# Batch 0 in two head sets and two token parts, one PSUM pool placed by hand, W_in's product in chunks, and a new order of all work

## The chip, the core and the metric

The kernel runs on one core of a Trainium2 chip. The metric is the device time of one execution in microseconds.

## The reference, cut to what matters

```python
def sm_attn(qq, kk, vv):
    s = scale * np.matmul(qq, kk.transpose(0, 1, 3, 2))
    a = np.exp(s - np.max(s, axis=-1, keepdims=True))
    a = a / (np.sum(a, axis=-1, keepdims=True) + 1e-09)
    return np.matmul(a, vv)

p_packed = sm_attn(p, k, v)              # p: 8 batches, 8 heads, 32 rows, 64 wide
out = sm_attn(q, p_packed, p_packed)     # q, k, v: 8 batches, 8 heads, 576 tokens, 64 wide
x = out.transpose(0, 2, 1, 3).reshape(4608, 512)
r = np.maximum(x @ w_in, 0.0)            # w_in: 512 x 2048
g = s * (r * r) + b                      # s, b: one number each
return g @ w_out                         # w_out: 2048 x 512
```

All inputs are fp32 in HBM. The first attention packs the 576 keys and values of a head into 32 rows; the second attends from the queries to these 32 rows.

## The kernel before

All loads of q, k, v, p and the weights are issued by GpSimd (POOL), whose DMA turns fp32 into bf16 on the way. The output's stores and the DMA transposes are issued by SyncE (SP). TensorE (PE), VectorE (DVE), ScalarE (ACT), POOL and SP each keep the order in which the program text names their instructions. That order is written out by hand as a string of words, which `run` turns into calls. For batch b the words are:

- Lk, Lq, Lv, Lp, Lwi, Lwo, Lpall, Lsb: loads of k, q, v, p, of a block of W_in's columns, of a quarter of W_out's rows, of the p of batches 2 to 7 at once, and of s and b.
- Tk, Tq: transposes of k and q by PE (batches 0 and 1), by halves of the heads. Dk, Dq: the same by DMA transpose (batches 2 to 7). PD, PP, PA, PPA: p is doubled and transposed into `pbd`.
- F: first scores and their exp, one of two head sets `a` at a time (heads 2g + a). V: v is put into the order of `vr` by DVE. P: the packed values with their sums, `pps`, then a reciprocal and two scalings into `pk`. X: `pk` transposed into `ppd`.
- S: second scores and exp (`e2`). A: column sums with `onesbd`, then ln and exp(-x) on ACT for the reciprocals, then the product on DVE, into `aT`.
- W: `ppd` times W_in, in chunks of 512 of W_in's 2048 columns, cast into `pw`. The attention's second product is folded into it: x @ W_in is `aT` times `pw`.
- M (h for the halves in batch 0): 128 columns of the hidden layer for all 576 tokens, four products of 288 columns, then a relu (ACT, sometimes DVE) and a square (DVE) into `gT`.
- O: steps of 512 output columns for 128 tokens, sixteen steps to an output tile (`yps`). At the sixteenth DVE multiplies by s, adds the bias row `biasrep`, and SP stores.
- BT, BC: W_out's column sums (16 products on 32-row strips), and a fp32 product with `rowsf` that adds the four strips and spreads them over the partitions, times b, into `biasrep`.
- Z, Y: products of a zero tile `zb`, results unused. Z goes to a tile of its own (`zps`), Y into the tile that the next step will use.

PSUM has two pools: `psh` (two buffers of two banks, tag h: scores, transposes, W pairs, M) and `psy` (four buffers of one bank: outputs, packed values, single W chunks). Which buffer a step gets follows from the order of requests. An M step occupies one `psh` buffer until its relu has read it.

Batch 0 goes by halves of 288 tokens and by halves of the heads. Its words:

```python
        Lwi0 Lwi1 Lwo0 Lwi2 Lwi3 Lwo1 Lp1 Tk0.0 Z10 PD Tk0.1 Lk1 PP0 Z3 F0.0 V0.0 F0.1 Z5 P0.0 V0.1 Lv1
        P0.1 Z1 Tq0.0 Z1 X0 Z1 Tq0.1 Lq1 Lwo2 Lwo3 Lpall Z3 S0 Z3 A0.0 Z1 W0.0 A0.1 G0.0 E Y8 h0.0.0
        G0.1 Z1 h0.2.0 Z1 W0.1 Y4 h0.2.1 Y1 h0.0.1 Y1 M0.4 M0.5 W0.2 M0.6 M0.7 W0.3 M0.8 M0.9 M0.10
```

Later batches interleave M steps of batch b with O steps of the batch before, mostly one or two of each in turn. In the profile nearly every ACT, DVE and POOL instruction bears line 73 and every matmul line 62 (transposes 65), the lines of the helpers that record them, so groups are told apart by the names of their tiles: hps is a `psh` tile, wps a single W chunk, rlu a relu's result.

Of the kernel before, what the change touches and what calls it, by code (L numbers as in the profile page):

```python
# [14 lines left out]
def kernel(  # L15
# [32 lines left out]
    JJ = NP // 16  # L48

# [8 lines left out]
    psh = ctx.enter_context(tc.tile_pool(name="psh", bufs=2, space=bass.MemoryType.PSUM))  # L58
    psy = ctx.enter_context(tc.tile_pool(name="psy", bufs=4, space=bass.MemoryType.PSUM))
# [17 lines left out]
    early = []  # L77

    def big(dt=F32):
        if early:  # L80
            return early.pop()
        return psh.tile([P, 2, NB if dt == F32 else 2 * NB], dt, tag="h", name="hps")
# [12 lines left out]
    pn = [constp.tile([P, 2, 2, D], BF16, name=f"pn{i}") for i in range(2)]  # L95
    pall = constp.tile([16 * (B - 2), 16, 2, D], BF16, name="pall")
# [10 lines left out]
    rowsf = constp.tile([P, P], F32, name="rowsf")  # L107
# [7 lines left out]
    def load(what, b, h0=0, h1=H):  # L115
        src = {"k": k, "q": q, "v": v}[what]
        if h0 == 0:
            raw[what, b] = rawp.tile([R, H, NC * D], BF16, tag=what + "n", name=what + "n")
        pool.dma_start(
            out=raw[what, b][:, h0:h1, :],  # L120
            in_=src[b, h0:h1].rearrange("h (r c) d -> r h (c d)", c=NC),
        )

# [21 lines left out]
    def load_sb():  # L145
        sp.dma_start(out=svec[:], in_=moe_s[0:1].unsqueeze(0).to_broadcast([P, 1]))
        sp.dma_start(out=bvec[:], in_=moe_b[0:1].unsqueeze(0).to_broadcast([P, 1]))
# [6 lines left out]

    def prep_p(b):
        pt = big(BF16)
        for x in range(2):
            tr(
                pt[:, 0, x * P:(x + 1) * P],
                pn[b][:, x, :, :],  # L160
                identb[:],
            )
        for c2 in range(2):
            act.copy(
                out=pbd[D * c2:D * c2 + D, :, b, :, c2, :],
                in_=pt[D * c2:D * c2 + D, 0, 0:2 * P].rearrange("p (g a j) -> p a g j", g=4, a=2),
            )

    def prep_pall():
        n = 16 * (B - 2)  # L170
        pts = [psy.tile([P, 8 * P], BF16, tag="y", name="pps") for _ in range(2)]
# [6 lines left out]
        for x in range(2):  # L178
            src = pts[x][:].rearrange("p (t n) -> p t n", n=P)[:, :, 0:n].rearrange(
# [9 lines left out]
    def on_pe(b, what, half):  # L189
        dst = (kT if what == "k" else qT)[b % 2]  # L190
        if what == "q":
            dst = dst[:].rearrange("p h c r -> p (h c r)")
        tpw = big(BF16)
        tp = [tpw[:, 0], tpw[:, 1]]
        split = b == 0 and what == "q"
        if split:
            tp[1] = psy.tile([P, 2 * NB], BF16, tag="y", name="tps")
        for h4 in range(4):
            for cp in range(CP):
                o = (h4 % 2) * HS + cp * R  # L200
                tr(
                    tp[h4 // 2][:, o:o + R],
                    raw[what, b][:, 4 * half + h4, cp * P:(cp + 1) * P],
                    identb[0:R, 0:R],
                )
        d = dst[:, half * 4 * HS:(half + 1) * 4 * HS].rearrange("p (a s) -> p a s", a=2)
        if split:
            act.copy(out=d[:, 0], in_=tp[0][:, 0:2 * HS])
            vec.tensor_copy(out=d[:, 1], in_=tp[1][:, 0:2 * HS])
        else:  # L210
            vec.tensor_copy(out=d, in_=tpw[:, :, 0:2 * HS])
# [8 lines left out]
    def order_v(b, h0=0, h1=H):  # L220
        vec.tensor_copy(
            out=vr[:, :, h0:h1, 0:D].rearrange("r c h d -> r h c d"),
            in_=raw["v", b][:, h0:h1, :].rearrange("r h (c d) -> r h c d", c=NC),
        )

    def first_scores(b, a):
        if a == 0:
            e1[b] = attp.tile([R, 2, NC, 4, NP], BF16, tag="e1", name="e1")
        s1 = big()
        for g in range(4):  # L230
            for cp in range(CP):
# [8 lines left out]
                )  # L240
        act.activation(
# [8 lines left out]
    def packed(b, half=None):  # L250

        if not half:
            pps[b] = psy.tile([P, NB], F32, tag="y", name="pps")
        pp = pps[b][:, 0:2 * DV].rearrange("p (a x) -> p a x", a=2)
        for a in range(2):
            for c in range(NC):
                for g in range(4) if half is None else (2 * half, 2 * half + 1):
# [8 lines left out]
        if half == 0:  # L266
            return
        rd = smp.tile([P, 2], F32, tag="rd", name="rd")
        vec.reciprocal(out=rd[:], in_=pp[:, :, D])
        pk[b] = smp.tile([P, 2, 2, D], BF16, tag="pk", name="pk")  # L270
        for a in range(2):
# [6 lines left out]
    def turned(b):  # L278

        pt = pps[b][:, NB // 2:].bitcast(BF16)  # L280
        for a in range(2):
            tr(pt[:, a * P:(a + 1) * P], pk[b][:, a].rearrange("p c d -> p (c d)"), identb[:])
        vec.tensor_copy(
            out=ppd[b % 2][:].rearrange("p a g j -> p (a g j)"),
            in_=pt[:, 0:2 * P],
        )

    def second_scores(b, by_half=False, with_w=False):
        e2[b] = attp.tile([P, 2, S], BF16, tag="e2", name="e2")
        tiles = [big() for _ in range(2)]  # L290
        for a in range(2):
            for g in range(4):
                for c2 in range(2):
                    t, i = (c2, a) if by_half else (a, c2)
                    mm(
                        tiles[t][NP * g:NP * g + NP, i, 0:HS],
# [6 lines left out]
        if by_half:  # L303
            exp_half(b, tiles, 0, 0)
            exp_half(b, tiles, 1, 0)
            s2[b] = tiles
            return
        if with_w:
            packed_w(b, [0])
        for a in range(2):  # L310
            act.activation(
# [6 lines left out]
    def exp_half(b, tiles, a, hf):  # L318
        act.activation(
            out=e2[b][:, a, hf * HS:(hf + 1) * HS],  # L320
            in_=tiles[hf][:, a, 0:HS],
            func=AF.Exp,
            scale=scale,
        )

    def weights_half(b, hf):
        if hf == 0:
            aT[b] = atp.tile([P, 2, S], BF16, tag="aT", name="aT")
        dps = big()
        for a in range(2):  # L330
            mm(dps[:, a, 0:HS], onesbd[:], e2[b][:, a, hf * HS:(hf + 1) * HS], start=True, stop=True)
        if hf == 0:
            exp_half(b, s2[b], 0, 1)
            exp_half(b, s2[b], 1, 1)
        ld = smp.tile([P, 2, HS], F32, tag="ld", name="ld")
        act.activation(out=ld[:], in_=dps[:, :, 0:HS], func=AF.Ln)
        rcd[hf] = smp.tile([P, 2, HS], F32, tag="rcd", name="rcd")
        act.activation(out=rcd[hf][:], in_=ld[:], func=AF.Exp, scale=-1.0)

    def weigh_half(b, hf):  # L340
        cols = slice(hf * HS, (hf + 1) * HS)
        vec.tensor_tensor(out=aT[b][:, :, cols], in0=e2[b][:, :, cols], in1=rcd[hf][:], op=ALU.mult)

    def weights(b, a):
        if a == 0:
            aT[b] = atp.tile([P, 2, S], BF16, tag="aT", name="aT")
        dps = big()
        for hf in range(2):
            mm(dps[:, hf, 0:HS], onesbd[:], e2[b][:, a, hf * HS:(hf + 1) * HS], start=True, stop=True)
        ld = smp.tile([P, 2, HS], F32, tag="ld", name="ld")  # L350
        act.activation(out=ld[:], in_=dps[:, :, 0:HS], func=AF.Ln)
        rc = smp.tile([P, S], F32, tag="rcd", name="rcd")
        act.activation(out=rc[:], in_=ld[:].rearrange("p a s -> p (a s)"), func=AF.Exp, scale=-1.0)
        vec.tensor_tensor(out=aT[b][:, a, :], in0=e2[b][:, a, :], in1=rc[:], op=ALU.mult)

    def packed_w(b, chs):
        if b not in pw:
            pw[b] = atp.tile([P, 2, DFF], BF16, tag="pw", name="pw")
        where = {}
        if len(chs) > 1:  # L360
            pair = [big() for _ in range(2)]
            where = {(a, x): pair[a][:, x, :] for a in range(2) for x in range(2)}
        if len(chs) != 2:
            single = [psy.tile([P, NB], F32, tag="y", name="wps") for _ in range(2)]
            where.update({(a, len(chs) - 1): single[a][:] for a in range(2)})
        for x, ch in enumerate(chs):
            for g in range(4):
                for a in range(2):
                    mm(
                        where[a, x][NP * g:NP * g + NP],  # L370
                        ppd[b % 2][D * a:D * a + D, a, g, :],
                        w_in_sb[D * a:D * a + D, g, ch * NB:(ch + 1) * NB],
                        start=True,
                        stop=True,
                        tile_position=(D * a, NP * g),
                    )
        if len(chs) > 1:
            for a in range(2):
                dst = pw[b][:, a, chs[0] * NB:(chs[0] + 2) * NB].rearrange("p (i f) -> p i f", f=NB)
                evict(dst, pair[a][:], a == 0)  # L380
        if len(chs) != 2:
            ch = chs[-1]
            if b == 0 and ch == 0:
                s2["w"] = single
                first_w(b, 0)
                return
            for a in range(2):
                evict(pw[b][:, a, ch * NB:(ch + 1) * NB], single[a][:], a == 0)

    def first_w(b, half):  # L390

# [329 lines left out]
```

The softmax here doesn't subtract the row's maximum and nothing guards it: scores larger than these inputs give would overflow.

## Time and profile before

| what | value |
|---|---|
| runs | 250.38, 250.39, 251.3 us; median 250.39 |
| span of the profiled execution | 248.0 us (no separate time is given for it; the median lies 2.4 above its span) |
| PE busy | 241.6 us, 2302 matmuls |
| DVE, ACT, POOL busy | 144.4, 140.6, 29.1 us |
| DMA | 35.50 MB moved; software queue (POOL's loads) 18.61 MB, hardware queue (SP's stores and transposes) 16.49 MB |
| relus on ACT, 576 columns | 124, mean 649 ns |
| casts of W pairs, 1024 columns | 14 on ACT, mean 1012 ns; 14 on DVE, mean 1220 ns |

The span runs from the first to the last instruction of the profiled execution. Busy time of PE is the sum of matmul durations, which overlap in the pipeline; a step's real cost is the distance between the starts of consecutive steps. MB of loads are counted as the bf16 that arrives, half of what is read.

### The profile page before, as it was taken

What the parts mean: (1) busy time and instruction counts of PE and PEld (TensorE: products, weight loads), DVE (VectorE), ACT (ScalarE), POOL (GpSimd) and SP (SyncE); (2) the same over time, 40 slices, a digit from 0 to 9 for tenths busy, and PEclk for the clock granted to TensorE, in tenths of its full rate; (3) what the DMA queues carried; (4) which work ended last, traced back from release to release, by engine and by line L of the source; (5) the groups of instructions that cost most, each with busy time, mean ns of one, the idle gap of its engine ahead of it and who ended that gap; (6) DMA issues with size and microseconds to landing.
All of it is one profiled execution on the core that took longest, in us unless ns stands there. A gap on an engine that the chain in (4) does not pass through costs nothing.

```text
span 248.0 us, 5518 instructions
## 1 busy us (share of the span) xinstructions
PE 241.6 (97%) x2302; PEld 134.2 (54%) x2302; DVE 144.4 (58%) x278; ACT 140.6 (57%) x218; POOL 29.1 (12%) x43
## 2 busy tenths in 40 slices
PE   8999899999999999999999999999999999999994
PEld 2655565356644665456544654466545654366453
DVE  4438875599564864386538753586348742767221
ACT  2266742558837772758555953888266844578000
POOL 8733212000300012000300030000200000000000
PEclk9999999999999999999999999999999999999999
DMA  6999999999696589939798999337998811121133
GB/s 74 174 206 208 201 203 204 197 204 162 136 213 140 140 138 144 225 89 193 115 209 169 160 147 226 85 80 156 146 230 133 185 37 50 42 46 42 42 87 86
DMA packets 59450, 35.50 MB, mean 143 GB/s; under 512 B 32160, under 2 KB 54944, under 8 KB 59424
## 3 DMA queue, kind: packets, MB, share of 16 engines
q0 software_dynamic: 25184, 18.61, 50.8%
q1 hardware_dynamic: 34192, 16.49, 30.2%
q8 instruction: 18, 0.29, 0.5%
q14 instruction: 8, 0.07, 0.1%
q10 hardware_dynamic: 48, 0.03, 0.0%
HBM read 37.23 MB, written 9.44 MB: 188 GB/s over the span
## 4 chain that ended last, share of the span: by engine, by line
PE 82%; DMA 16%; issue 1%; POOL 0%; DVE 0%; POOLq 0%
PE yps L62 49%; PE hps L62 31%; DMA w_out_sb<-in_moe_w_out_dram 14%; DMA kn<-in_k_dram 2%; PE pps L62 1%; PE pps L65 1%; POOL kn L73 0%; DVE ysb L73 0%; POOL identb L73 0%; POOLq L73 0%; POOLq L705 0%
## 5 line engine op out<-in xcount | busy, mean ns | idle before, releaser
L62 PE MATMUL yps<-w_out_sb,gT 128*128 128x512 bf16 (+1 forms) x592 | 147.8, 374 | 0.6 <-DMA w_out_sb<-in_moe_w_out_dram 0.6
L73 ACT ACTIVATE rlu<-hps 128x576 bf16<-128x576 f32 x124 | 77.0, 649 | 23.1 <-PE hps L62 19.9
L62 PEld LDWEIGHTS <-gT 128*128 128x128 bf16 x592 | 54.8, 98 | 50.9 <-issue 8.8
L62 PE MATMUL hps<-aT,pw 128*128 128x288 bf16 x512 | 78.3, 285 | 0.2 <-ACT rlu L73 0.2
L73 DVE TENSOR_TENSOR gT<-rlu 128x576 bf16<-128x576 bf16 x128 | 57.8, 457 | 26.1 <-ACT rlu L73 23.3
L62 PEld LDWEIGHTS <-pw 128*128 128x128 bf16 x512 | 49.7, 97 | 26.3 <-issue 1.2
L73 DVE SCALAR_TENSOR_TENSOR ysb<-yps,svec,biasrep 128x512 f32<-128x512 f32 (+1 forms) x37 | 27.0, 733 | 21.7 <-PE yps L62 21.5
L73 ACT ACTIVATE e<-hps 96x768 bf16<-96x768 f32 (+2 forms) x34 | 21.8, 693 | 30.8 <-PE hps L62 30.6
L73 ACT CAST pw<-hps 128x1024 bf16<-128x1024 f32 x14 | 14.2, 1012 | 21.6 <-PE hps L62 21.0
L73 DVE TENSOR_TENSOR aT<-e,rcd 128x576 bf16<-128x576 bf16 x16 | 12.1, 757 | 23.4 <-ACT rcd L73 23.2
L73 POOL DMA_DIRECT2D kn<-in_k_dram x9 | 6.9, 767 | 130.1 <-DMA kT<-kn 97.8
L73 DVE CAST pw<-hps 128x1024 bf16<-128x1024 f32 x14 | 17.1, 1220 | 4.7 <-PE hps L62 4.6
L62 PE MATMUL zps<-zb 128*128 128x512 bf16 x42 | 13.6, 452 | 1.2 <-DVE zb L73 1.2
L73 ACT ACTIVATE rcd<-ld 128x576 f32<-128x576 f32 x16 | 10.9, 683 | 0.5
L73 ACT ACTIVATE ld<-hps 128x576 f32<-128x576 f32 x16 | 10.3, 643 | 1.2 <-PE hps L62 0.4
L62 PEld LDWEIGHTS <-ppd 64*32 64x32 bf16 x384 | 3.8, 88 | 11.0 <-issue 8.1
L62 PEld LDWEIGHTS <-zb 128*128 128x128 bf16 x56 | 5.6, 108 | 7.2 <-issue 3.2
L73 DVE RECIPROCAL rd<-pps 128x2 f32<-128x2 f32 x8 | 1.4, 171 | 13.3 <-PE pps L62 13.3
L62 PE MATMUL hps<-w_in_sb,ppd 64*32 64x512 bf16 x224 | 8.9, 381 | 0.0
L62 PEld LDWEIGHTS <-kT 128*128 128x128 bf16 x192 | 6.9, 98 | 2.5 <-issue 0.5
L73 DVE COPY vr<-vn 96x3072 bf16<-96x3072 bf16 (+1 forms) x9 | 8.0, 893 | 0.1
L73 POOL DMA_DIRECT2D vn<-in_v_dram x9 | 6.7, 751 | 5.5 <-DVE vr L73 2.9
(58 smaller groups left out, 104.0 us busy)
## 6 DMA issues: line engine op xcount, KB each, us to landing
out_dram<-ysb SPq DMA_DIRECT2D x23, 192.0 KB, 2.6
kn<-in_k_dram POOLq DMA_DIRECT2D x7, 576.0 KB, 7.1
vn<-in_v_dram POOLq DMA_DIRECT2D x7, 576.0 KB, 10.7
qn<-in_q_dram POOLq DMA_DIRECT2D x7, 576.0 KB, 13.3
out_dram<-ysb SPq DMA_DIRECT2D x24, 128.0 KB, 2.4
w_in_sb<-in_moe_w_in_dram POOLq DMA_DIRECT2D x4, 512.0 KB, 14.3
w_out_sb<-in_moe_w_out_dram POOLq DMA_DIRECT2D x4, 512.0 KB, 18.7
out_dram<-ysb SPq DMA_DIRECT2D x23, 64.0 KB, 2.1
```

The source lines that it names most:

```text
L62: return tc.keep_in_program_order(nc.tensor.matmul(*a, **kw))
L65: return tc.keep_in_program_order(nc.tensor.transpose(*a, **kw))
L73: return lambda *a, **kw: tc.keep_in_program_order(f(*a, **kw))
```

## The change

- Batch 0's k and v are loaded, transposed and scored by head sets `a` rather than by halves of the heads, so that F, P and X of set 0 need only the first half of each load. P and X are done set by set.
- Batch 0's q is cut by tokens: `PARTS` gives 384 tokens (two of the three 128-wide pieces of each head's row) and 192 tokens. The load, the transposes, second scores, exp, sums, ln, inverse, weighing and h steps go by these parts, each with its own word (S, e, d, l, i, G, h).
- p0 is loaded as fp32 by SP and cast while doubled (`twice_p0`). s and b are loaded by POOL, late, instead of by SP at the start.
- PSUM is one tile of eight banks, `banks`; a word's `@n` says which bank or banks its step takes.
- Each step is a generator: its first word issues the PE part, further words issue the parts on ACT or DVE one at a time, with `a` or `v` choosing the engine. So evictions, relus, squares and output evictions (Q) have places of their own in the order.
- W goes by single chunks: 256 columns for batch 0, 512 for others, each with two casts of 512 (or 256) columns. W_in is loaded in five pieces: columns 512 to 1024, 1024 to 1536, 0 to 256, 1536 to 2048, 256 to 512.
- BC is gone: DVE adds the four strips of BT into `bias4` and multiplies them by b into the four strips of `biasrep`, eight instructions.
- Z is left at 12 + 3 + 2 + 1 + 5; Y is gone. All words are in a new order. Among the loads, k1, v1 and q1 are now ahead of all of W_out, and W_out's second half follows k2. M steps of batch 1 stand among the O steps of batch 0; those of later batches stand closer together. Dk of the next batch is mostly ahead of or far from Dq.

```diff
+    PARTS = ((0, 2), (2, 3))
...
-    psh = ctx.enter_context(tc.tile_pool(name="psh", bufs=2, space=bass.MemoryType.PSUM))
-    psy = ctx.enter_context(tc.tile_pool(name="psy", bufs=4, space=bass.MemoryType.PSUM))
+    psp = ctx.enter_context(tc.tile_pool(name="psp", bufs=1, space=bass.MemoryType.PSUM))
...
+    banks = psp.tile([P, 8, NB], F32, name="banks")
+    spots = []
+    def take(n, dt=F32):
+        x = spots.pop(0)
+        t = banks[:, x:x + n, :]
+        return t if dt == F32 else t.bitcast(dt)
...
+            x = slice(PARTS[part][0] * P, PARTS[part][1] * P)
+            pool.dma_start(
+                out=raw["q", 0][:, :, x],
+                in_=q[0].rearrange("h (r c) d -> r h (c d)", c=NC)[:, :, x],
+            )
...
+            out=raw[what, 0][:, 4 * part:4 * part + 4, :],
+            in_={"k": k, "v": v}[what][0].rearrange("(g a) (r c) d -> a r g (c d)", a=2, c=NC)[part],
...
+    def load_p0():
+        sp.dma_start(out=p0f[:], in_=p[0].rearrange("(x g) j d -> (g j) x d", x=2))
...
+    def scores0(u, a):
+        cols, w = part(u)
...
+        for g in range(4):
+            for c2 in range(2):
+                mm(
+                    s2[u][NP * g:NP * g + NP, c2, a * w:(a + 1) * w],
+                    ppd[0][D * c2:D * c2 + D, a, g, :],
+                    qh[D * c2:D * c2 + D, head(a, g), cols],
...
+    def packed_w(b, ch):
...
+        t = take(2)
+        cols = slice(ch * NB, (ch + 1) * NB)
+        for g in range(4):
             for a in range(2):
-                dst = pw[b][:, a, chs[0] * NB:(chs[0] + 2) * NB].rearrange("p (i f) -> p i f", f=NB)
-                evict(dst, pair[a][:], a == 0)
...
+            to((yield), pw[b][:, a, cols], t[:, a, :])
...
-        vec.tensor_copy(out=biasrep[:], in_=ps[:, 0, :])
-    def bias_rows():
-        ps = big()
-        mm(ps[:, 0, :], rowsf[:], biasrep[:], start=True, stop=True)
-        vec.tensor_scalar_mul(out=biasrep[:], in0=ps[:, 0, :], scalar1=bvec[:])
+        yield
+        vec.tensor_copy(out=bias4[:], in_=ps[0:NP, 0, :])
+        for g in range(1, 4):
+            vec.tensor_tensor(out=bias4[:], in0=bias4[:], in1=ps[NP * g:NP * g + NP, 0, :], op=ALU.add)
+        for g in range(4):
+            vec.tensor_scalar_mul(out=biasrep[NP * g:NP * g + NP], in0=bias4[:], scalar1=bvec[0:NP])
...
-    run("Lsb")
+    run("Lp0")
...
-    idle(12, NB)
+    run("Z12@7")
     for word in """
...
+        Lq0.1 PD0 PP0@1 PP0a Z3@0 Tk0.0@2 PP0a Lp1 Tk0.0a Tk0.0a Z2@0 Tk0.1@4 Tk0.1a Tk0.1v F0.0@6
+        F0.1@0 V0.0 F0.0 V0.1 Lwi2.4 Z1@3 P0.0@2 P0.0 Z5@6 X0.0 X0.0v F0.1 P0.1 Tq0.0@4 P0.1 Tq0.0a X0.1
+        Tq0.1@3 S0.0.0@6 X0.1a Tq0.0v S0.0.1 Lwi4.6 PD1 Lwi0.1 PP1@2 Tq0.1v Tq0.1v e0.1 S0.1.0@0 S0.1.1
+        e0.0 e1.0 d0.1@4 d1.0@6 e1.1 d1.1 l0.1 l1.0 i1.0 l1.1 i1.1 W0.3@0 W0.3v G1.0 d0.0 W0.2@6 i0.1
+        W0.3v l0.0 i0.0 Lwi6.8 G1.1 h0.6.1@0 W0.2v h0.6.1v h0.6.1 W0.5@4 W0.2a W0.5a W0.5v h0.4.1@6
...
+        h0.12.0 Lsb h0.0.0@6 h0.0.0a Lwo0.4 P1.1@4 P1.1 h0.14.1 h0.0.0 h0.10.0@2 h0.2.0a h0.10.0a
+        h0.8.1@6 h0.8.1a X1 X1v Tq1.0@0 Tq1.1@4 Tq1.0v Tq1.0a W1.0@2 W1.0a Tq1.1v Tq1.1v S1@6,0 W1.0v
+        W1.2@4 O0.1x1@2 h0.2.0 S1 O0.3x1@3 S1 A1.0@6 A1.0 A1.0 W1.2v W1.2v O0.3x2 h0.8.1 O0.1x1 O0.3x1
+        A1.1@0 W1.1@4 A1.1 A1.1 W1.3@6 O0.1x1 Lwo4.8 O0.3x1 W1.3a O0.2x2@0 O0.1x1 O0.3x1 O0.2x1 h0.10.0
+        A1.0 O0.2x1 W1.3v A1.1 M1.12@6 Lpall PA O0.2x3 W1.1v W1.1a Lk2 M1.7@4 M1.7v M1.12a O0.1x1
...
+        M1.10@6 M1.10a O0.0x1@1 O0.3x1 M1.7 PPA0@4,5 PPA0 O0.3x1 Lwo8.12 M1.6@6 M1.6v O0.2x1 M1.10
+        O0.0x2 M1.6 M1.12 O0.1x1 O0.0x2 O0.1x1 PPA0 O0.3x1 PPA0 M1.1@6 O0.1x1 O0.3x1 Lwo12.16 BT@4
+        O0.1x3 M1.1a M1.1 O0.1x1 Dk2 O0.3x4 O0.1x3 F2.1@6 F2.1 O0.1x1 Lv2 BT Q0.1 O0.2x3 F2.0@4 F2.0
+        M1.4@6 V2 M1.4a O0.2x2 M1.4 O0.2x1 M1.9@4 M1.9a Lq2 M1.9 M1.0@6 M1.0a M1.0 P2.1@2 P2.1 M1.3@4
...
```

## The prediction

> **What bounds the kernel now.** I read the page first, then PE's waits, the chain, PE's timeline and the DMA view by stages. PE is busy 97% of the span, but part of that is filler (products of the zero tile zb), so the share says little.
>
> ```profile
> span 248.0 us, 5518 instructions
> PE 241.6 (97%) x2302; PEld 134.2 (54%) x2302; DVE 144.4 (58%) x278; ACT 140.6 (57%) x218; POOL 29.1 (12%) x43
> ...
> L62 PE MATMUL zps<-zb 128*128 128x512 bf16 x42 | 13.6, 452 | 1.2 <-DVE zb L73 1.2
> ```
>
> The groups with their shapes kept apart show 14 more, into a tile of the next step:
>
> ```profile
> L62 PE MATMUL hps<-zb 128*128 128x512 bf16 x14 | 3.7, 379 | 0.0
> ```
>
> 56 fillers: 12 ahead of the first load (1.19 to 6.29 us, 0.43 us each) and 44 later. The chain has this as its long early pieces:
>
> ```profile
> 2.42 5.81 DMA kn<-in_k_dram
> 8.51 14.02 DMA w_out_sb<-in_moe_w_out_dram
> 22.81 19.50 DMA w_out_sb<-in_moe_w_out_dram
> ...
> 228.15 16.46 PE yps L62 x92
> ```
>
> So up to 42.3 us the end is set by loads that reach W_out late, afterwards by PE alone. The stretches (length, PE, PEld, DVE, ACT, POOL busy, granted clock, DMA share, GB/s) show that the queue never rests there:
>
> ```profile
> 12.00:18.00 6.00, 5.93 (x107) 3.24 (x105) 2.24 (x7) 3.61 (x9) 2.23 (x3) 1.00 1.27 206
> ...
> 36.00:42.00 6.00, 5.78 (x115) 3.73 (x113) 4.60 (x10) 2.16 (x3) 1.54 (x2) 1.00 1.27 206
> ```
>
> 206 GB/s is the load limit of the first 50 us. PE's timeline gives what a step costs, as the distance of starts (start, length, what):
>
> ```profile
> 59.84 0.38 PE L62 MATMUL yps<-w_out_sb,gT 128*128 128x512 bf16 x1
> 60.05 0.65 PE L62 MATMUL hps<-aT,pw 128*128 128x288 bf16 x4
> 60.54 0.38 PE L62 MATMUL yps<-w_out_sb,gT 128*128 128x512 bf16 x1
> ...
> 70.83 0.81 PE L62 MATMUL yps<-w_out_sb,gT 128*128 128x512 bf16 x3
> 71.57 0.63 PE L62 MATMUL hps<-w_in_sb,ppd 64*32 64x512 bf16 x16
> 72.13 1.47 PE L62 MATMUL yps<-w_out_sb,gT 128*128 128x512 bf16 x6
> ```
>
> An O step is 0.216 us (in the last 16.46 us: 60 of these and 32 half ones of 0.11), an M 0.49, two W chunks 0.56, and going from a full to a tiled shape costs 0.09 more (70.83 + 3 x 0.216 = 71.48, next start 71.57), back likewise.
>
> **What the Trainium skill says.** "TensorE: Matmul & The Clock Gate", Part 1: the array runs at half clock until some 3.4 us of activity, and falls back after an idle window of that length. The first fillers agree (0.43 against 0.216 us); no gap of before is long enough to show the fall. "DMA: Bandwidth & Descriptors", Queues, rings and completion order: each DMA engine goes round-robin over the queues, packet by packet. No run here shows a DMA transpose beside loads: before, they start after 56 us, when loads pause. "Perfetto Trace Analysis", Optimizing Scalar/DVE Operations: half of an ACT or DVE instruction's latency overlaps with the next. The trace agrees: two relus back to back take 1.19 us, not 2 x 0.65, so ACT's pace is 0.54.
>
> **The change on PE, counted.** The order of after, by these steps: O 124.5 us, h and M 62.7, W 7.9, F 5.6, P and S 6.9, column sums 3.9, all transposes 5.9, BT 0.95, 66 shape changes 6.0, filler after the first twelve 2.4 (11 x 0.216). Sum 226.9, after the same start at 6.3. Before by the same count: 235.4, of which filler 9.5 (44) and the fp32 bias product 1.1. The count is good: from batch 2's first scores (67.05) on it gives 178.2, the trace 177.6. From 6.3 it gives 241.7 where the last matmul ended at 244.6; 1.6 of that 2.9 are PE's waits (two DMA waits of 0.6, two ACT waits of 0.2). So 8.5 us of PE work go. Were PE never to wait, it would end at 233. It will wait, since removed filler stood where PE had nothing to do.
>
> **When the loads let it go on.** The second half of q0 landed at 14.6 (issue 5.8, 8.8 to landing). After it the new queue carries p1, w_in columns 512 to 1536, 0 to 256, 1536 to 2048, k1, w_in 256 to 512, v1, q1, s and b (now here, two small ones), W_out blocks 1 and 2, pall, k2, blocks 3 and 4, v2, q2. k, v, q are 0.59 MB each, W_in and W_out 2.1 each. At 205.5 GB/s from 14.6, 0.5 us for the receipt, 0.2 to 0.7 for the smaller pieces of q0 and W_in and for s and b (estimates). "Ahead" is counted PE work before the first use, "left" the work after it:
>
> - q1: lands 34.3, ahead 20.3, left 206.6: PE ends no earlier than 240.9
> - W_out 1: 37.0, 22.3, 204.6: 241.6
> - W_out 2: 39.6, 25.0, 201.9: 241.5
> - W_out 3: 46.3 to 47.3, 32.2, 194.7: 241.0 to 242.0
> - W_out 4 (13th matmul of BT): 48.8 to 50.8, 34.2, 192.7: 241.5 to 243.5
>
> The two ends for 3 and 4: k2 lands at about 43.7, before them, and Dk2 is SP's second instruction, with no store ahead of it, so its transpose runs beside them. Its packets busied the engines some 2 us when alone (the landing took 5.0). Nil is possible, 2 us if it takes its full share; I take 1, so 49.8. Dk2 itself lands at 49 to 53; its F2.1 has 36.8 ahead, so needs it at 52.4: just covered. Dq2 (q2 at 55 to 56.5, plus 6 to 8) against S2 at 63.6: just covered; both would cost at most 1.
>
> **The chain of batch 0.** k0's first half lands at 5.9 as before; p0 goes by SP, ahead of all stores, and its pair of transposes and pbd are done by 7.2. Head set 0: T until 7.7, two ACT copies (0.64 each) 9.05, F 9.5, exp (0.80) 10.5, vr half (v0 at 10.1) 10.9, P 11.3. DVE then waits in order for v0's second half (11.6) and its 0.7 copy, so rd and pk come at 12.9, X 13.5, set 1's pk 14.1. q0 at 13.5 and 15: second scores 15.4 to 16.4, then ACT in order: four exps, ln, inverse (eight of 0.3 to 0.5) to 19.5, first h at 19.9, against 20.37 now. 8.3 is ahead of it, so it allows an end at 238.5: 3 us of slack under the loads. The head sets and the 384/192 cut therefore bring nothing by themselves. Idle PE from 12 to 20 could drop to half clock; some 4 us of work at half speed is 2 us, inside that slack.
>
> **ACT and DVE.** Splitting W casts in two costs 2 x 0.588 + 2 x 0.684 against 1.01 + 1.22, 0.3 a batch, beside PE; singly placed W chunks add shape changes, counted. From the first h to 44 us DVE has some 22 us of work in 24 by full durations, so it is nearly full, but the loads come later still. Bias: POOL's two issues and SP's two are exchanged with p0's and cost nothing visible. BT's sums now go through DVE: 0.68 + 3 x 0.75 + 4 x (0.4 to 0.75) = 4.5 to 5.9 us. Queued behind are output 0.1's eviction and V2 (0.95), for which P2.1 waits on PE. BT ends on PE at about 50.8, V2 is done at 56.5 to 58.5, and P2.1 (40.6 ahead) is due at about 56.4: I add 0.5, with 0 and 2 as ends. PSUM: M now rotates through three pairs of banks instead of two, which excludes a loss there as long as ACT keeps pace; I credit no gain, since the old waits were 0.2.
>
> **Sum.** 49.8 + 192.7 x 0.996 (the count's own error) + 0.5 = 242.2 for PE's end, 2.4 less than 244.6. The tail (half eviction, store, 3.4) stays: span 245.6. The page has no separate time for its execution; the runs are 250.38 to 251.3, median 250.39, so 2.4 lies around the span, and I keep it: **248.0 us**.
>
> **Rivals.**
> - Loads a little better: Dk2 delays nothing, V2 is covered: PE ends at 241.0, 246.8 us. For it: 2 us of transposing is little. Chance 0.23; the forecast as worked out 0.43.
> - The filler comes back as waiting: Dk2 takes its share, W_out 4 lands at 51.5 to 53, or V2 is late by 2: PE ends at 243.7 to 245.3, 249.3 to 250.9 us. For it: six loads have bounds within 1 us of each other, so any slip is paid at once. Chance 0.17, mostly inside 0.5% (1.25 us, about what a measurement here can tell from no change).
> - Slower: ACT becomes the bound in the M runs of batches 3 to 7. These now come nearly unbroken (16 M with some ten O steps, 10.2 us of PE), after inverses and W casts are left to ACT just before (3.1 us). At 0.65 a relu ACT needs 12.8, less 1.5 that three bank pairs hold: 1 us a batch, 5 in all on top of the forecast, 253. It decides from about 0.60 a relu; 1.19 for two speaks for 0.54 and against it. Chance 0.17.
> - The change does not do what it says: the transposes are not clear of loads, since Dk2 runs amid them. That is the second rival's cause, not counted again.
>
> **Numbers.** Faster 0.68 (the first two, and a little of the third), same 0.13, slower 0.19. The forecast's own range is 246 to 249.2; to leave out no more than 2 in 10 the range goes to the third case and into the fourth: 245.8 to 251.4.
>
> **What would show it.** Right: PE's busy sum lower by about 8 us while the span falls by 2 to 3; PE waits on DMA of w_in, kn, qn and w_out between 20 and 50 us, together over 6 us; W_out's last landing at 49 to 51; no PE wait worth naming after 65. Wrong: W_out's last landing before 47 or after 52.5; PE waiting for ACT rlu more than 1 us in all after 85; a granted clock under 1 beyond 25 us; P2.1 waiting over 2 us on DVE vr.

## The result and the profile after

The changed kernel is slower: 257.81 us median (255.88 to 259.47) against 250.38 of the kernel before in the same job, a ratio of 1.0287 with a 95% interval of 1.0231 to 1.0342. The profiled execution took 255.88 us, its span is 254.1. Where the runs of a kernel below fall into two groups, its median covers all of them and its ratio the faster group only; for k2_pe_best there is no ratio, and its profile is of a run of the slower group.

The page's lines that answer to those shown of before (the last one is the row of granted clock in 40 slices):

```profile
span 254.1 us, 5614 instructions
...
PE 237.9 (94%) x2315; PEld 134.0 (53%) x2315; DVE 152.5 (60%) x312; ACT 133.4 (52%) x237; POOL 30.6 (12%) x45
...
PEclk9995999985999999999999999999999999999999
```

PE is busy 3.7 us less, but the span is 6.1 longer, and the clock is low in two places. The chain of work that ended last (start, length, what) shows which:

```profile
36.91 6.84 PE banks L62 x68
43.75 14.20 DMA kT<-kn
57.95 0.05 issue
57.99 3.37 PE banks L62 x29
61.37 11.19 DMA qT<-qn
72.55 0.04 issue
72.60 33.18 PE banks L62 x283
```

No W_out load is in it. Two DMA transposes are: Dk2, issued at 43.75 and landed 14.2 us later, and Dq2, 11.2 us. In the kernel before the same two landed 5.4 and 6.5 us after their issue and ended nothing. From 72.60 on PE runs without a wait that the profile lists to its last matmul at 250.22: 177.6 us, where the forecast's count of this stretch gives 178.2. So the whole loss of this execution lies before 72.6. PE's waits between 48 and 80 us (total, times, longest):

```profile
PE banks L62 <- DMA kT<-kn: 5.4, 1, 5.4
PE banks L62 <- DMA qT<-qn: 1.1, 1, 1.1
```

And the stretches, with the columns of before (length, PE, PEld, DVE, ACT, POOL busy, granted clock, DMA share, GB/s):

```profile
12.00:18.00 6.00, 4.41 (x104) 2.63 (x104) 2.50 (x9) 4.08 (x12) 3.02 (x5) 1.00 1.38 201
18.00:24.00 6.00, 5.34 (x42) 2.58 (x43) 4.37 (x12) 3.82 (x11) 1.51 (x3) 0.51 1.30 203
36.00:42.00 6.00, 5.91 (x77) 2.72 (x75) 5.86 (x13) 5.94 (x11) 0.77 (x1) 1.00 1.53 197
54.00:60.00 6.00, 2.01 (x16) 1.18 (x17) 1.66 (x4) 0.81 (x1) 0.77 (x1) 0.64 0.71 75
60.00:66.00 6.00, 6.00 (x88) 3.91 (x87) 2.98 (x9) 3.03 (x5) 0.77 (x1) 0.79 1.10 169
```

PE's O steps before the wait end at 52.57. The counted work from there to S2 is 11.2 us; it took 20.0. The difference of 8.8 is 5.4 and 1.1 of waiting, and 2.3 lost since PE ran at half clock from 58.0 to 62.5.

Much of why a transpose takes 14 us is seen in the DMA view of 48 to 53 us (queue, packets, MB, share; q0 carries the loads, q1 Dk2 alone here):

```profile
q0 software_dynamic: 943, 0.71, 90.6%
q1 hardware_dynamic: 944, 0.24, 36.3%
```

One packet of the transpose leaves for each packet of the loads of v2 and q2, 189 a microsecond each. A transpose of 0.59 MB is 2304 packets of 256 bytes; a load packet there has 768. At 189 a microsecond 2304 packets need 12 us, however little of the bandwidth they use. Dk2's needed less, since the loads thinned out at about 54. Its 14.2 us are 4.0 to the first packet, 6.6 beside the loads, 3.1 for the rest and 0.5 from the last packet to the landing. Turns do not explain the 3.1: from 55 to 58 only 72 load packets stand beside 731 of the transpose, and both queues together move 77 GB/s, while in held_loads (below) 1132 packets of Dk2 alone pass in the microsecond from 49 to 50. Nor do they explain why the first packet leaves 4.0 us after the issue, where Dq of the kernel before needs 1.2 to 1.7. Both stay open.

The same view of the kernel before, 57 to 65 us, has no line of q0:

```profile
q1 hardware_dynamic: 4884, 1.53, 112.6%
...
qT<-qn SPq DMA_TRANSPOSE x1, 6.5
kT<-kn SPq DMA_TRANSPOSE x1, 5.4
```

No load packet falls between the first and the last packet of any of its twelve transposes. In the changed kernel Dk3 and Dk4 ran beside loads too (8.1 and 7.4 us), but nothing on PE waited for them.

### The profile page after: what moved, and what is told of

It reads as the page before. It is cut to its first block, busy times and chain, and to the rows that moved or that the text cites. A ratio compares the mean times of both kernels' runs of the same rounds, so it can differ in the third digit from the quotient of the medians.

```text
span 254.1 us, 5614 instructions
## 1 busy us (share of the span) xinstructions
PE 237.9 (94%) x2315; PEld 134.0 (53%) x2315; DVE 152.5 (60%) x312; ACT 133.4 (52%) x237; POOL 30.6 (12%) x45
## 4 chain that ended last, share of the span: by engine, by line
PE 79%; DMA 15%; POOL 2%; ACT 1%; issue 1%; DVE 0%; POOLq 0%; ACTq 0%
PE banks L62 79%; DMA kT<-kn 6%; DMA w_in_sb<-in_moe_w_in_dram 5%; DMA qT<-qn 4%; ACT rlu L73 1%; POOL qn L73 1%; POOL kn L73 1%; POOL vn L73 1%; PE banks L65 0%; POOL w_in_sb L73 0%; POOL pn L73 0%; ACT qT L73 0%; DVE ysb L73 0%; POOL identb L73 0%; POOLq L73 0%
## 5 line engine op out<-in xcount | busy, mean ns | idle before, releaser
L62 PE MATMUL banks<-w_out_sb,gT 128*128 128x512 bf16 (+1 forms) x592 | 142.6, 376 | 0.0
L73 ACT ACTIVATE rlu<-banks 128x576 bf16<-128x576 f32 (+2 forms) x113 | 67.5, 661 | 25.7 <-PE banks L62 23.1
L62 PE MATMUL banks<-aT,pw 128*128 128x288 bf16 (+2 forms) x512 | 77.2, 293 | 1.0 <-DVE aT L73 0.7
L73 DVE TENSOR_TENSOR gT<-rlu 128x576 bf16<-128x576 bf16 (+2 forms) x128 | 55.9, 455 | 20.4 <-ACT rlu L73 15.5
L73 DVE SCALAR_TENSOR_TENSOR ysb<-banks,svec,biasrep 128x512 f32<-128x512 f32 (+1 forms) x37 | 26.8, 733 | 43.6 <-PE banks L62 40.6
L73 ACT ACTIVATE e<-banks 96x768 bf16<-96x768 f32 (+3 forms) x34 | 21.9, 694 | 50.3 <-PE banks L62 50.3
L73 DVE CAST pw<-banks 128x512 bf16<-128x512 f32 (+1 forms) x38 | 23.1, 628 | 10.9 <-PE banks L62 10.9
L73 ACT CAST pw<-banks 128x512 bf16<-128x512 f32 (+1 forms) x34 | 16.3, 549 | 2.1 <-PE banks L62 2.1
L73 DVE TENSOR_TENSOR aT<-e,rcd 128x576 bf16<-128x576 bf16 (+2 forms) x18 | 12.0, 684 | 3.2 <-ACT rcd L73 3.2
L62 PE MATMUL banks<-w_in_sb,ppd 64*32 64x512 bf16 (+1 forms) x288 | 11.7, 366 | 1.2 <-DMA w_in_sb<-in_moe_w_in_dram 0.6
L73 ACT ACTIVATE rcd<-ld 128x576 f32<-128x576 f32 (+2 forms) x18 | 10.8, 629 | 0.3
## 6 DMA issues: line engine op xcount, KB each, us to landing
w_out_sb<-in_moe_w_out_dram POOLq DMA_DIRECT2D x4, 512.0 KB, 15.5
```

Of the source, the lines that this page charges most:

```text
L62: return tc.keep_in_program_order(nc.tensor.matmul(*a, **kw))
L73: return lambda *a, **kw: tc.keep_in_program_order(f(*a, **kw))
```

## The experiments

Theory A: the two transposes run beside loads, land late, and PE's waiting then halves its clock. Theory B: the half clock of batch 0 (18 to 25 us) is the loss. In the diffs `...` stands for words left out, and what follows `#` is a remark.

**k2_on_pe, k2q2_on_pe.** Batch 2's transposes move from the DMA to PE, k's alone or q's with it.

```diff
-        BT@4 O0.1x3 M1.1a M1.1 O0.1x1 Dk2 O0.3x4 O0.1x3 F2.1@6
+        Tk2.0@6 O0.1x1 Tk2.0a Tk2.0v ... BT@4 M1.1@6 M1.1a O0.1x3 M1.1 Tk2.1@6 O0.1x1 Tk2.1a Tk2.1v O0.3x4 O0.1x3 F2.1@6
# k2q2_on_pe only:
-        O0.0x1 Dq2 PPA0 X2
+        O0.0x1 Tq2.0@4 PPA0 X2 O0.0x3 Tq2.0a Tq2.0v ... M1.5 Tq2.1@6 O0.3x1 Tq2.1a Tq2.1v
```

> The changed kernel with k of batch 2 transposed by PE (as k of batch 1 is) in place of the DMA transpose Dk2; nothing else is taken out. Theory A (Dk2 shares the DMA engines with the loads of v2 and q2, lands at 58.0 and not at 49 to 53, and the 5.4 us of waiting then halve PE's clock for 57 to 63 us): the wait for kT (5.4) and the slow stretch (some 2.4 us of work lost) go, 1.0 us of transposes and 0.2 of shape changes come. The q transpose Dq2 stays, and k3's load can now start earlier and run beside it, so its wait of 1.1 may grow to 3. PE ends at 250.2 - 7.8 + 1.2 = 243.6, up to 245.6 with the q wait; 249.3 to 251.3 us. Theory B (the half clock of 18 to 25 us in batch 0 is what was lost, and the wait at F2.1 only shows it): the wait goes, another takes its place; 254 us or more.

> As k2_on_pe, and q of batch 2 by PE as well, so that no DMA transpose stands before batch 3. Theory A: also the wait of 1.1 for qT goes, another 1.2 of PE work comes: PE ends at 243.7, 249.4 us (248.9 to 250.5), no PE wait over 1 us between 45 and 75 us, granted clock 1.00 from 26 us on. Theory B: 254 us or more.

Measured: 256.25 us, 1.0228 (1.0196 to 1.0259), and 251.45, 1.0027 (1.0007 to 1.0046). With both on PE 6 of the 7 us are gone, with the clock of 18 to 24 us as low as it was (0.53): theory A holds, and theory B falls as the main cause. With k2 alone on PE the wait for kT goes, but the one for qT grows from 1.1 to 3.8, more than I allowed for. SP's timeline says why:

```profile
59.11 1.17 SPq L73 DMA_DIRECT2D out_dram<-ysb  x2
60.42 6.63 SPq L73 DMA_TRANSPOSE qT<-qn  x1
```

Dq2 stands in SP's queue behind Q0.1's two stores; these wait for DVE's bias chain. q2's last load packets had left by 54.5. Issued only at 60.4, Dq2 then meets v3's load and lands 10.8 us later.

**fill_wait, fill_early.** Filler is put back, ahead of the wait or into batch 0's gaps.

```diff
-        O0.3x4 O0.1x3 F2.1@6
+        O0.3x4 O0.1x3 Z24@6 F2.1@6                    # fill_wait
-        S0.1.1 e0.0 e1.0 d0.1@4 d1.0@6 e1.1 d1.1 l0.1
+        S0.1.1 Z2@3 e0.0 e1.0 d0.1@4 Z1@3 d1.0@6 Z1@3 e1.1 d1.1 Z2@3 l0.1    # fill_early, and five products more
```

> The changed kernel with 24 products of the zero tile (5.2 us at 0.216) on PE just ahead of batch 2's first scores, where PE waits for kT; the transposes stay. Theory A splits its loss in two, waiting 5.4 and slow clock 2.4: the clock stays at 1.00 from 26 us on, F2.1 still starts at 58, PE ends at 247.8, 253.5 us. If the slow clock after the wait costs nothing on the path: 255.9 as the profiled run of the changed kernel.

> The changed kernel with ten products of the zero tile (2.2 us at full clock) placed singly and in twos between 14.7 and 19.5 us, where PE's short gaps stand ahead of the fall of the clock at 18.2 us. Theory A: the clock stays at 1.00 through batch 0 and PE reaches BT up to 3 us earlier than 49.0 (or waits for W_out), but F2.1 waits for kT until 58 all the same; 255 to 258 us, no gain, and the wait for kT grows from 5.4 to 7 or 8 us. Theory B: 3.4 us of half-speed work are won, 252.5 us.

Measured: 258.23 us, 1.0285 (1.0222 to 1.0347), and 256.09, 1.0212 (1.0182 to 1.0242). In fill_wait the clock stays at 1.00 from 55 to 64 us and F2.1 starts at 58.2 as before, yet nothing is won: the wait moves to the next transpose, and the clock falls there instead (72.6 to 76.0).

```profile
PE banks L62 <- DMA qT<-qn: 3.7, 1, 3.7
```

Dq2 lands at 73.2 there (72.55 in the changed kernel), so S2 cannot start earlier. Waiting and slow clock were not two terms to be added: behind both stood a second late transpose. fill_early adds eleven products, not the ten that I wrote. Its clock is low from 11.0 to 14.4 us, ahead of this filler, and then at 1.00 up to the wait for kT; so half of the slow stretch is gone, not all. BT starts at 49.45 against 49.03 and the wait for kT is 5.3. I had expected BT up to 3 us earlier. Later in batch 0 DVE and ACT are nearly full (5.86 and 5.94 of 6 us between 36 and 42 in the changed kernel), which speaks against PE's clock setting the pace there. The 252.5 of theory B did not come. Its 1.7 us below the changed kernel's median can't be told from nothing; the intervals overlap.

**before_load_beside.** The suspected cost is added to the kernel before.

```diff
-        Tq1.0 Tq1.1 Lq2 X1
+        Tq1.0 Tq1.1 Lq2 Ldum X1
+            pool.tensor_copy(out=junk[:], in_=raw["q", 2][0:1, 0, 0:2])     # Ldum: when q2 has landed,
+            pool.dma_start(out=dum[:], in_=moe_w_out[0:12 * P, :].rearrange("(m p) d -> p m d", p=P))
```

> The kernel before, with one load more: 1536 rows of W_out (1.5 MB as bf16) into a tile that nobody reads, issued once q2 has landed (about 55 us), so that it runs beside Dq2 and Dk2, which have no load packet beside them in the kernel before. Theory A (a transpose's 256-byte packets get one turn for each load packet, and its first packet leaves 4 us after its issue and not 1.2): beside the load Dq2's packets come at 150 to 190 per us, Dq2 lands at 67 to 69 and not at 62, Dk2 at 70 to 72 and not at 65; F2.0, due at 67, waits about 4, the clock falls if the wait is over 3: 254.5 to 256.5 us. If only bandwidth is shared (2304 packets of 256 bytes are 0.6 MB, 3 us at 206 GB/s): Dk2 lands by 67, 250.4 to 251.

Measured: 258.58 us, 1.0307 (1.0283 to 1.033). One idle load of 1.5 MB makes the kernel before as slow as the changed one. As in the changed kernel the packets go one for one (DMA view of 66 to 69 us):

```profile
q0 software_dynamic: 456, 0.47, 91.2%
q1 hardware_dynamic: 456, 0.12, 29.4%
```

SP's timeline and PE's wait:

```profile
56.92 9.06 SPq L73 DMA_TRANSPOSE qT<-qn  x1
66.10 6.11 SPq L73 DMA_TRANSPOSE kT<-kn  x1
```

```profile
PE hps L62 <- DMA kT<-kn: 6.5, 1, 6.5
```

At 206 GB/s the load takes 7.5 us, but SP's issue of Dq2 alone takes 9.1 instead of 2.9, Dk2 is behind it, and F2.0 starts at 74.3 and not at 67. The clock falls in this wait of 6.5 us as well (0.54 from 72 to 78). It is 2 us worse than I expected; had only bandwidth been shared, I expected no loss.

**k2_pe_q2_early, held_loads.** Two ways to clear the transposes.

```diff
# k2_pe_q2_early: k2_on_pe, and
-        Lv2 BT Q0.1 O0.2x3 ... M1.9a Lq2 M1.9 ... O0.0x1 Dq2 PPA0
+        Lv2 Lq2 BT Dq2 Q0.1 O0.2x3 ... M1.9a M1.9 ... O0.0x1 PPA0
# held_loads: fill_early, and (GK, GQ: POOL copies two elements of kT, of qT)
-        Dk2 O0.3x4 ... M1.11 Lk3
+        Dk2 GK O0.3x4 ... M1.11 GQ Lk3
```

> As k2_on_pe (256.25 us; PE waits 3.8 for qT there), with the one remaining transpose Dq2 put ahead of Q0.1 in SP's order, so that it no longer stands behind that store, which waits for DVE's bias chain (Dq2 was issued at 60.4 while q2's last load packet left at about 54). Theory A (late issue behind the store, then k3's and v3's loads beside it): issued at 54 to 55, landed by 63, ahead of the need at 67; the wait of 3.8 and about 1.2 of slow clock after it go: 251.2 us. If the issue time is not what made it late (it runs beside k3's load in any case and takes 11 again): landing 65 to 66, still ahead of the need, same time. If S2 is held by something else: 255 or more.

> As fill_early (256.1 us), both DMA transposes kept, but POOL reads two elements of kT ahead of Lv2 and two of qT ahead of Lk3, so that v2 and q2 are loaded only when Dk2 has landed, and k3 only when Dq2 has. Theory A: Dk2 has no load beside it after 47 us, takes 5 to 6 and lands at 49 to 50; no wait for kT at F2.1; v2 lands at 55 to 56 (P2.1 needs it at 57), q2 at 58 to 59, Dq2 at 64 to 65 against S2 at about 63.7: a wait of about 1. PE ends at 65 + 177.6 = 242.6 to 243.3, 248.6 to 249.5 us. Theory B (DMA transposes here are late for another reason than the loads, as SP or the descriptors): Dk2 lands at 58 as before, 256 or more.

Measured: 250.26 us, 0.9981 (0.9967 to 0.9995), and 251.95, 1.0043 (1.0024 to 1.0062). Dq2, issued at 54.2, is landed well ahead of S2 at 66.6, no wait for qT is left, and 6 us are won over k2_on_pe by the place of one transpose in SP's order (q2's load goes ahead with it, but keeps its place in POOL's order). In held_loads both transposes stay on the DMA and the wait for kT is gone all the same: Dk2 has 120 load packets between its first and last instead of 1349 (those of 768 bytes or more), lands by 51.0, and F2.1 starts at 51.6. fill_early, the same without the holds, had Dk2 land after 14.2 us, so it was the loads that made it late. But holding has a price of its own, which I set too low:

```profile
PE banks L62 <- DVE vr L73: 4.6, 1, 4.6
```

v2's load, issued at 51.6, landed at 59.0, not 55 to 56: the load queue had run dry, and its first packet left at 53.1.

**k2_pe_best.** k2_pe_q2_early with the early filler and V2 ahead of BT's sums.

> As k2_pe_q2_early, with the ten early zero products of fill_early and V2 ahead of the bias sums in DVE's order. P2.1's wait for vr (1.1) goes, and the half clock of 12 to 25 us, which in k2_on_pe put BT at 49.9 where the loads allow about 48: another 1 to 2.5 us. 249 us (248.3 to 250.5); no PE wait over 0.6 us between 45 and 75.

Measured: 255.06 us median of four, 250.53 to 256.11. The hoped-for 249 did not come. V2 ahead of BT's sums only moved the wait: F2.0 now waits 1.2 for these sums. S2 starts at 66.4, no later than in k2_pe_q2_early, so batch 2 is not what was lost. At 183 us PE waits 2.9 for DVE pw, behind V7, whose v7 is late, and the clock is then low from 185.6 to 192.4, which costs 3.4; together that is the loss against k2_pe_q2_early's profiled run (256.11 and 249.89). Dk6 had been issued at 156.99, q7's load at 157.22. The DMA view of 161 to 165 us:

```profile
DMA packets 627, 0.18 MB, mean 45 GB/s; under 512 B 588, under 2 KB 627, under 8 KB 627
...
q1 hardware_dynamic: 587, 0.15, 126.4%
q0 software_dynamic: 40, 0.03, 6.5%
```

The engines count as busy and move 45 GB/s; here the median packet of Dk6 took 100 to 156 ns, against 18 to 31 over other transposes. Dk6 landed 14.6 us after its issue. An issue close together is not enough for this: in fill_wait q7's load follows Dk6 after 0.4 us and in k2_pe_q2_early after 1.0, and Dk6 lands after 8.0 and 8.4 us.

**k2_pe_bias_early.** What was left between F2.1 and S2 was DVE: in k2_pe_q2_early P2.1 waited 1.1 us for vr, and V2 stood behind the bias sums. To clear DVE, the second copy of kT also goes to ACT.

```diff
-        BT@4 M1.1@6 M1.1a O0.1x3 M1.1 Tk2.1@6 O0.1x1 Tk2.1a Tk2.1v O0.3x4 ... Lv2 Lq2 BT Dq2 Q0.1 ... V2
+        Lv2 BT@4 M1.1@6 M1.1a O0.1x3 BT Tk2.1@6 O0.1x1 Tk2.1a Tk2.1a V2 M1.1 O0.3x4 ... Lq2 Dq2 Q0.1
```

> As k2_pe_q2_early (250.26 us; P2.1 waits 1.1 there for vr, F2.0 0.3 for the bias sums), with DVE's order alone changed: BT's eight instructions stand where BT's products end (about 50.2 us) and not after the second half of kT's copies (52.7), that copy goes to ACT, and V2 comes right after BT. Theory (the bias chain of 4.7 us on DVE, queued ahead of V2 and of Q0.1, is the rest of what the forecast missed): P2.1 starts at 57.5 to 58 and not at 59.3, S2 at 64.5 to 65.5 and not at 66.6, 248.6 us (248.0 to 249.3). If PE between F2 and S2 is held by ACT or by the banks instead: 250.3 as before.

Measured: 248.66 us, 0.9923 (0.9903 to 0.9944), with one of six runs at 251.95. P2.1 no longer waits (58.55, 8.4 after BT's start against 10.1) and the time is as expected, though in the profiled run BT itself came 0.9 later and S2 at 65.9.

**k2_pe_bias_all, k2_pe_all_held.** The early filler again, and q7's load held until Dk6 has landed; then k3, q3 and v5 held in the same way, until Dq2, Dk3 and Dk4.

```diff
-        W5.0@6 Lq7 A5.1 ... Dk6 O4.1x1
+        W5.0@6 A5.1 ... Dk6 GK Lq7 O4.1x1              # k2_pe_bias_all
-        M1.11 Lk3 ... M2.9@2 Lq3 ... M3.1 Lv5
+        M1.11 GQ Lk3 ... M2.9@2 GH Lq3 ... M3.1 GK Lv5    # k2_pe_all_held (GH: two elements of kT[1])
```

> As k2_pe_bias_early, with the ten early zero products of fill_early, and q7's load held until Dk6 has landed (in k2_pe_best q7's load ran beside Dk6, which took 13 us, and v6's successor v7 came late: 2.9 us of waiting and a slow clock at 183 to 192 us). Theory A: the early clock is worth at most 0.4 (BT at 48.7 against 49.2), the hold removes the slips of 5 us that k2_pe_best showed in three of four runs: 248.3 us (247.6 to 249.3), no run over 250.5. If those slips have another cause, some runs are at 253 to 256.

> As k2_pe_bias_all, whose 22 runs fall into two groups, 14 at 247.2 to 250.9 and 8 at 253.1 to 255.0 us. Four loads are now held, each until the transpose that stands beside it has landed: k3 until Dq2, q3 until Dk3, v5 until Dk4, q7 until Dk6 (the last as there). If a load that starts beside a transpose is the cause of the slow group (in k2_pe_best's profile q7's load was issued 0.2 us after Dk6, and for 8 us the two moved some 40 GB/s together): no run above 251, median 247.6 (247.0 to 248.6). If the slow group has another cause: again a third of the runs at 253 to 255.

Measured: k2_pe_bias_all 249.85 us median, 14 of 22 runs at 247.2 to 250.9 (0.9936, 0.9916 to 0.9956) and 8 at 253.1 to 255.0: one hold does not remove the slips. k2_pe_all_held 247.96 us, five runs within 247.82 to 248.21, 0.9896 (0.988 to 0.9911). With these four loads held no run of five is above 248.3. But at the rate of k2_pe_bias_all (8 of 22) five runs without a slip would come by luck one time in ten. Nor are all transposes clear: v5's load, held until Dk4 has landed, now starts just ahead of Dq4, which lands after 9.4 us. And the early filler is a rival: k2_pe_q2_early, without it and with no load held, has no run above 251.4 in twenty. So it is not shown that the loads cause the slips. The page of k2_pe_all_held:

```profile
span 246.2 us, 5664 instructions
...
PEclk9999999999999999999999999999999999999999
```

Its median is the lowest of all, 2.6 us under the kernel before and 10 under the changed one; its interval overlaps that of k2_pe_bias_early.

**before_no_filler.** The forecast's ground, that filler only fills.

```diff
-        Tk0.0 Z10 PD Tk0.1 Lk1 PP0 Z3 F0.0 V0.0 F0.1 Z5 P0.0
+        Tk0.0 PD Tk0.1 Lk1 PP0 F0.0 V0.0 F0.1 P0.0            # and all other Z and Y words after the first
```

> The kernel before without its 44 later zero products (Z and Y words; the first twelve stay). The forecast took it that removed filler stood where PE had nothing to do, so that it comes back as waiting for loads: 250.4 us within 0.5, with PE waits on DMA before 45 us larger by 5 to 8 us. If the clock falls in the gaps as it does in the changed kernel at 18 us and batch 0 has no slack for it: 251.5 to 253 us. If the filler cost time: 248 to 249.5.

Measured: 250.95 us, 1.0019 (1.0009 to 1.003). 9.5 us of PE work are gone and the time is 0.5 longer. The clock is low from 9 to some 26 us:

```profile
PEclk9755899999999999999999999999999999999999
```

So filler was no cost and its removal no gain. I had expected 5 to 8 us more of waiting for DMA ahead of 45 us; that grew from 1.2 to 2.1 only, waiting for ACT and DVE from 0.4 to 4.4, and products ran slower.

## Why the prediction was wrong

**The step that failed** is "Dk2 itself lands at 49 to 53", with "both would cost at most 1". It landed at 57.95, and Dq2 at 72.55 where S2 was due at 63.6. I sized the transpose by the engine time that it takes alone ("busied the engines some 2 us when alone"), a few lines below the sentence of the Trainium skill ("DMA: Bandwidth & Descriptors", Queues, rings and completion order) on which it turns: each DMA engine goes round its queues packet by packet. The page means a bundle of descriptors by a packet, and no run shows how the profile's packets relate to these, so the sentence alone gives no price. The trace agrees with it in the counts, 943 to 944. I looked only at what Dk2 would do to the loads and gave that 0 to 2 us; it did nothing to W_out, since its first packet left at 47.7, when W_out was all but in. For what the loads would do to Dk2, the landing at 49 to 53 allowed 5.3 to 9.3 us after the issue at 43.7; the issue came at 43.75 and the landing took 14.2.

**The order behind it.** Dq2 was forecast for 55 to 56.5 and 6 to 8 us. q2 landed at 57.2, and Dq2 was issued at 61.4, since it stood behind Q0.1's stores, and those behind the very wait for kT. I had listed what SP's queue holds ahead of Dk2, not ahead of Dq2.

**The clock.** That batch 0 could fall to half clock "inside that slack" fits fill_early, where less of it brought BT no earlier. That a wait of 5 us would halve the clock a second time was not considered. Its cost was hidden by Dq2 (fill_wait); a clock under 1 beyond 25 us was named as a sign of error and was one.

**What held.** W_out's first use at 37.6 (37.0 forecast), BT at 49.03 (49.1, from the 49.8 of its 13th product), and 177.6 us from S2 on (178.2). The first two are in part luck, since the reason given did not hold: the profile lists no wait of PE for a load between 20 and 50 us, where over 6 us were forecast. Products at half clock up to 25 us and nearly full DVE and ACT later stand in their place, and W_out's last block landed at 48.89, before BT's 13th product. The bias chain on DVE took 4.8 us (50.13 to 54.95; 4.5 to 5.9 forecast). The changed kernel hid it; with the transposes cleared its place in DVE's order was worth some 1.5 us (0.9981 to 0.9923 of the kernel before), inside the 0 to 2 given and above the 0.5 taken. "PE's busy sum lower by about 8" was 3.7, since half-clock products count double. The tail was 3.9 and the time around the span 1.8, where 3.4 and 2.4 had been taken; these cancel.

**The rivals.** ACT as a bound did not come: after 74 us PE has no wait that the profile lists. "The filler comes back as waiting: Dk2 takes its share" named the right cause and the wrong victim: not W_out was late, but the transpose. That the transposes run amid loads was noted as a fact and priced as nothing of its own; it was the slower case I should have worked out. With it cleared and nothing else (k2_pe_q2_early) the kernel runs at 250.26, with 1.2 us more of PE work, and so level with the kernel before. The 247.96 of k2_pe_all_held took DVE's new order, the early filler and held loads besides. That the rest of the change is worth the 2.4 us forecast is therefore not shown.

What stays open: why the changed kernel's own runs spread over 3.6 us, why a transpose's first packet leaves so late beside loads, and what made Dk6 and q7's load crawl in k2_pe_best.

## What to carry to other kernels

Size a DMA beside another by turns, not by bytes: count its packets, divide by the rate at which the other queue's packets pass, and add the late start (4 us here). A transpose of small packets took 1.7 to 2.6 times as long beside loads as alone (Dq2 and Dk2); put it where the loads pause, make later loads wait for it, or give it to PE if the pause costs more. And for each transfer read what stands ahead of it in its issuing queue: one early wait can hold the next transfer back and bring it into the next load.

## What the runs showed of the hardware

- A DMA transpose of 0.59 MB: 2304 packets. For Dq in the kernel before, with no load beside, the first packet left 1.2 to 1.7 us after the issue; beside loads in the changed kernel 3.97 for Dk2 and 4.25 for Dq2. Landing after 4.4 to 6.5 us (the twelve of before), and 14.2 and 11.2 for these two. SP's own time for it is 2.4 to 3.6 us in the kernel before, 7.5 for Dk2 in the changed one.
- In the changed kernel the granted clock fell at 55.7 us, 3.1 after the end of PE's last product, and came back 4.5 us after work began again at 58.0. Over the seven profiles in which PE waited 2.9 us or more after 50 us, it fell 2.4 to 5.2 us after that end. The Trainium skill gives an idle window of about 3.4 us ("TensorE: Matmul & The Clock Gate", Part 1); the measured times lie on both sides of it. Stretches at half clock lasted 3.4, 6.8, 13.7 or 17.1 us, all multiples of 3.4, when the kernel's end did not cut them off. But the clock also fell at 18.2 us, with no gap over 0.65 us: PE was busy 4.4 of the 6 us ahead. With eleven products more there (fill_early) it did not fall at 18.2, though it had been low from 11.0 to 14.4.
- A transpose and a load issued 0.2 us after it (k2_pe_best): 45 GB/s together from 161 to 165 us, and landings after 14.6 and 15.5 us. Seen in one profile.
